# A fused retention and gated-experts kernel: the norm's last step on ScalarE, the masked scores in front of the normalised rows, operand tasks open to two engines, zero matmuls between the first scores

## The chip, the cores and the metric

The kernel runs on one core of one Trainium2 chip. The core has TensorE (PE in the profile; its weight loads are the separate row PEld), VectorE (DVE), ScalarE (ACT), GpSimd (POOL) and SyncE (SP, which issues most DMAs here). The metric is the device time of one execution in microseconds; lower is better. The kernel before was timed in three runs: 880.64, 884.82 and 885.79 us, median 884.82.

## The reference

Three stages, one after the other. Only the first stage and its passage to the second are touched by the change.

```
state = gamma * state + k[t] v[t]^T          # 2 batches, 8 heads, 768 steps, head_dim 64
y[t]  = scale * q[t] state

x  = y as (1536 tokens, 512)
xn = x / sqrt(mean(x*x) + 1e-6) * rms_g
x  = (silu(xn @ w_gate) * (xn @ w_val)) @ w_out           # 512 -> 1536 -> 512

p   = domain_probs / (sum(domain_probs) + 1e-9)           # 4 experts
out = sum over e of p[:, e] * (relu(x @ w1[e]) @ w2[e])   # 512 -> 1024 -> 512
```

## The kernel before

**Stage one, the retention.** A batch of 768 steps is cut into 6 chunks of 128; the two batches give 12 chunks, 0 to 11. For each chunk `scores` (L600) makes the 128x128 products of k and q for 8 heads into two PSUM banks. `masked` (L608, on DVE) multiplies them with decay and causality into the tile am. `mix` adds two products in one bank: q with the carried state S (L620, not in the first chunk of a batch) and am with v (L628). It then updates the state on PE (L654, operand kn scaled at L578 on POOL or DVE) and copies it to S on ACT (L661). The scaling of q (L589) is a task of POOL or DVE too.

**The norm.** In `mix`, ACT squares the 128x512 result with a running sum ss (L640), takes r0 = sqrt(ss/512 + eps) (L642) and vv = ss/512 + eps (L644). In `normal`, DVE takes r1 = 1/r0 (L668) and improves it by one Newton step, r1 * (1.5 - 0.5 * vv * r1 * r1), in three instructions on one column (L671 to L673). In `normal2`, DVE makes the normalised rows xn = y * r1 * rms_g (L680). `to_x` has PE transpose xn (L702) and lets ACT, DVE and POOL turn the result into operands of stage two.

**The passage to stage two.** Every float32 operand of stage two is split into a high part (a cast on ACT) and a low part (a subtraction on POOL or DVE), and each product is three matmuls: hi*hi, hi*lo, lo*hi (L447). Stage two is done by a 2x2 block scheme with 7 products, so that sums of blocks are wanted as well (tsum, L724 to L736). The operand tiles are xX, xB22 and xT, each with a hi and a lo tile. A group of chunks 0 to 5 feeds token half 0, chunks 6 to 11 token half 1. Weights arrive as 64-bit floats and are turned into float32 by ACT (L299) and DVE (L302 to L320), summed (L336) and split (L364, L369) by ACT, DVE and POOL.

**What sets the order.** There is no automatic scheduling here: the program writes out each engine's queue. Work that is not bound to a place is a task of the class Pace, which holds estimated costs and engine clocks. `pace.fill(span)` issues waiting tasks that its estimate says would end within the span; `pace.need(task)` issues a task now. A task names the engines that it may run on: "P" is POOL, "PV" is POOL or DVE, whichever the estimate has free first. Once issued, each engine runs its queue strictly in the order written. Loads are issued on SP in program order, behind the buffers that they refill (q and v have 3 buffers, k and kn 2).

**One iteration i of the main loop** loads chunk i+2, does `normal` and `normal2` of chunk i-1, `scores` and `masked` of chunk i+1, a fill, `mix` of chunk i, a fill, `to_x` of chunk i-1 and a last fill. The last two chunks are normalised directly behind their own mix. In iteration 10 the first products of stage two stand on PE behind `to_x` of chunk 9. Before the loop, 8 matmuls on zeros (L772, into the bank called idle) run while the first loads are under way.

Of the kernel before, what the change touches and what calls it, by code (L numbers as in the profile page):

```python
# [7 lines left out]
F32 = mybir.dt.float32  # L8
# [3 lines left out]
AF = mybir.ActivationFunctionType  # L12
ALU = mybir.AluOpType
PSUM = bass.MemoryType.PSUM

P = 128
# [3 lines left out]
EPS = 1e-6  # L20
# [131 lines left out]
def tile_retention_gated_experts(  # L152
# [27 lines left out]
    nc = tc.nc  # L180
    B, NCH = qt.shape[:2]
    H = c_k.shape[2]
    S = NCH * CHUNK
    NT, DM = out.shape
    DFF = w_gate.shape[1]
    E, _, F = w1.shape
    D = DM // H
    NTT = NT // P
    NP = H // 2
# [33 lines left out]
    pace = Pace({"A": nc.scalar, "V": nc.vector, "P": nc.gpsimd, "D": nc.sync})  # L223
# [311 lines left out]
    with ExitStack() as actx:  # L535
        ac = actx.enter_context(tc.tile_pool(name="ac", bufs=1))
# [9 lines left out]

        rows = [wstage.tile([P, H, CHUNK], F32, tag="wst", name=f"rows{x}")[0:1] for x in range(2)]
        g_sb = ac.tile([P, DM], F32, name="g_sb")
        eps = ac.tile([P, 1], F32, name="eps")
        table = ac.tile([P, 1], F32, name="table")  # L550

        S_sb = [ac.tile([P, NP, CHUNK], F32, name=f"S{x}") for x in range(2)]
# [2 lines left out]
        NS = len(chunks)  # L555
# [55 lines left out]
        def mix(i):  # L611
            b, c = chunks[i]
            yf = bank()
            if c:
                pace.matmuls(0, pace.need(st[i]["q task"]))
            y = yf.rearrange("p (h d) -> p h d", h=H)
            vt, am = st[i]["v"].rearrange("p (h d) -> p h d", h=H), st[i]["am"]
            for n in range(NP):
# [8 lines left out]
                for j in range(2):  # L627
# [4 lines left out]
                        start=not c,  # L632
                        stop=(j == 1) or not c,
                    )
            pace.matmuls(2.53 if c else 1.65, st[i]["v end"], st[i]["am end"], st[i].get("S end", 0.0))
            xn = ap2.tile([P, DM], F32, tag="xn", name="xn")
            ss, vv, r0, r1, r2 = (
                ap2.tile([P, 1], F32, tag=nm, name=nm) for nm in ("ss", "vv", "r0", "r1", "r2")
# [2 lines left out]
            end = pace.did("A", DM + 100)  # L641
            nc.scalar.activation(out=r0, in_=ss, func=AF.Sqrt, scale=1.0 / DM, bias=eps)  # L642
            end = pace.did("A", 1, end)
            nc.scalar.activation(out=vv, in_=ss, func=AF.Identity, scale=1.0 / DM, bias=eps)  # L644
            pace.did("A", 1)
            if c + 1 < NCH:

                if c == 0:
                    st[i]["state"] = pairs(psum_sum.tile([P, 512], F32, name="state"))
                d = st[i]["state"]  # L650
                pace.matmuls(0, pace.need(st[i]["k task"]))
                ks, vs = pairs(st[i]["kn"]), pairs(st[i]["v"])
                for n in range(NP):
                    nc.tensor.matmul(  # L654
                        out=d[:, n, :], lhsT=ks[:, n, :], rhs=vs[:, n, :], start=(c == n == 0), stop=True,
                        skip_group_check=True,
                    )
                pace.matmuls(0.87)
                new = S_sb[c % 2]
                for r in (slice(0, D), slice(D, P)):  # L660
                    nc.scalar.copy(out=new[r, :, r], in_=d[r, :, r])  # L661
                    s_end = pace.did("A", DM // 2)
                st[i + 1]["state"], st[i + 1]["S"], st[i + 1]["S end"] = d, new, s_end
            st[i]["norm"] = yf, xn, ss, vv, r0, r1, r2, end

        def normal(i):
            yf, xn, ss, vv, r0, r1, r2, end = st[i]["norm"]
            nc.vector.reciprocal(out=r1, in_=r0)  # L668
            end = pace.did("V", 1, end)

            nc.vector.scalar_tensor_tensor(out=r2, in0=r1, scalar=vv, in1=r1, op0=ALU.mult, op1=ALU.mult)  # L671
            nc.vector.tensor_scalar(out=r2, in0=r2, scalar1=-0.5, scalar2=1.5, op0=ALU.mult, op1=ALU.add)
            nc.vector.tensor_tensor(out=r1, in0=r1, in1=r2, op=ALU.mult)  # L673
            for _ in range(3):
                end = pace.work("V", 1, end)
            st[i]["r"] = xn, yf, r1, end

        def normal2(i):
            xn, yf, r1, end = st[i]["r"]
            nc.vector.scalar_tensor_tensor(out=xn, in0=yf, scalar=r1, in1=g_sb, op0=ALU.mult, op1=ALU.mult)  # L680
            st[i]["xn"], st[i]["xn end"] = xn, pace.did("V", DM, end)
# [4 lines left out]
        def split(g, readers, dep, hi, lo, t, size, last=False):  # L686

            high = pace.add(1, "A", size, lambda eng: eng.copy(out=hi, in_=t), dep)
            low = pace.add(
                1, "PV" if last else "P", size,  # L690
                lambda eng: eng.tensor_tensor(out=lo, in0=t, in1=hi.bitcast(F32), op=ALU.subtract), [high],
            )
            readers += [high, low]
            x_tasks[g] += [high, low]

        def to_x(i):
# [8 lines left out]
            if blk == 0:  # L705
# [22 lines left out]
            nc.vector.tensor_tensor(out=lo, in0=b22, in1=hi.bitcast(F32), op=ALU.subtract)  # L728
            pace.did("V", DM // 2, end)
            third = pace.add(  # L730
                1, "PV" if i == NS - 1 else "P", DM // 2,
                lambda eng: eng.tensor_tensor(out=t3, in0=t2, in1=b1[:, 0:KH], op=ALU.subtract), [done],
            )
            fourth = pace.add(
                1, "PV" if i == NS - 1 else "P", DM // 2,
                lambda eng: eng.tensor_tensor(out=t4, in0=b1[:, KH:KD], in1=t2, op=ALU.subtract), [done],  # L736
            )
            first_block[b, "readers"] += [third, fourth]
# [4 lines left out]
        def early(i):  # L743
            return i >= NS - 2

        man = tc.manual_schedule()
        man.__enter__()
        nc.gpsimd.memset(eps, EPS)

        nc.scalar.activation(out=table, in_=eps, func=AF.Sqrt)  # L750
        for x in range(2):
# [36 lines left out]
        for i in range(NS):  # L788
# [13 lines left out]
                nc.sync.dma_start(out=p_raw, in_=probs.rearrange("(t p) e -> p t e", p=P))  # L802
            if i and not early(i - 1):
                normal(i - 1)
                normal2(i - 1)
            if i + 1 < NS:
                scores(i + 1)
                masked(i + 1)
                pace.fill(1.15)
            mix(i)  # L810
            pace.fill(2.53)
            if i + 2 < NS:
                load(i + 2, "kn")
            if early(i):
# [326 lines left out]
```

## Time and profile before

| | us |
|---|---|
| median of 3 runs | 884.82 |
| lowest and highest run | 880.64, 885.79 |
| the profiled execution, whole | 882.98 |
| its span, first to last instruction | 881.2 |
| PE busy | 857.9 (97%) |
| PEld, DVE, ACT, POOL busy | 800.5, 593.5, 359.7, 296.2 |
| mean granted clock of TensorE | 0.981 |

The profile is of one execution. "Busy" is time in which an engine has an instruction in work; a wait is charged to what released it. The granted clock is the share of full speed that TensorE had: 1.00 is 2.4 GHz, 0.50 is 1.2 GHz. Between 0 and 112 us of the span lie the retention and the passage to stage two; after that PE is nearly always busy.

### The profile page before, as it was taken

How to read it: one execution, taken by the hardware profiler on the slowest of the kernel's cores; microseconds unless marked ns; L12 is line 12 of the kernel's file. 1: busy time of each engine (PE TensorE's matmuls, PEld its weight loads, DVE VectorE, ACT ScalarE, POOL GpSimd, SP SyncE). 2: the span in 40 equal slices, each digit the busy share in tenths (PEclk: the TensorE clock that was granted, in tenths of full speed). 3: DMA queues.
4: the chain of work that ended last, by engine and by line, in shares of the span. 5: the costliest groups of instructions: out<-in, count | busy, mean ns of one | idle time of the engine just before them, and what ended most of it. 6: DMA issues, size and time to landing. Idle time of an engine off the chain costs nothing.

```text
span 881.2 us, 12572 instructions
## 1 busy us (share of the span) xinstructions
PE 857.9 (97%) x4710; PEld 800.5 (91%) x4710; DVE 593.5 (67%) x1093; ACT 359.7 (41%) x786; POOL 296.2 (34%) x365
## 2 busy tenths in 40 slices
PE   9996899999999999999999999999999999999998
PEld 8886899999999999989899998899998899988997
DVE  3989789999788774872655566565656556565554
ACT  1654545545354544665342333333233333333221
POOL 2755534536374655951220120122112012111000
PEclk7978899999999999999999999999999999999999
DMA  7842022223121210010111010011011001101003
GB/s 277 286 151 85 25 72 79 89 72 96 49 86 59 73 48 25 25 37 13 48 37 35 26 48 26 23 49 36 13 47 49 25 25 49 36 13 48 25 1 144
DMA packets 33410, 53.96 MB, mean 61 GB/s; under 512 B 4419, under 2 KB 13507, under 8 KB 33349
## 3 DMA queue, kind: packets, MB, share of 16 engines
q1 hardware_dynamic: 33200, 53.01, 18.9%
q8 instruction: 37, 0.61, 0.3%
q14 instruction: 25, 0.20, 0.1%
q10 hardware_dynamic: 148, 0.14, 0.0%
HBM read 50.00 MB, written 3.15 MB: 60 GB/s over the span
## 4 chain that ended last, share of the span: by engine, by line
PE 82%; DVE 11%; POOL 3%; ACT 2%; issue 2%; DMA 1%; SPq 0%; DVEq 0%; ACTq 0%
PE bank L447 39%; PE bank L1022 10%; PE bank L1023 10%; PE bank L1021 10%; PE bank L955 3%; PE bank L954 3%; PE bank L953 3%; PE bank L628 1%; DVE s L880 1%; DVE sums L336 1%; DVE top L320 1%; POOL x2Tlo L906 1%; DVE kept L877 1%; DVE am L608 1%; DVE widelo L369 1%
## 5 line engine op out<-in xcount | busy, mean ns | idle before, releaser
L1029 DVE SCALAR_TENSOR_TENSOR oacc<-bank,p_sb,oacc 128x512 f32<-128x512 f32 (+1 forms) x181 | 134.9, 746 | 66.5 <-PE bank L1023 66.5
L1023 PE MATMUL bank<-plainhi,hs 128*128 128x512 f32 (+1 forms) x386 | 151.1, 391 | 0.0
L1022 PE MATMUL bank<-plainlo,hs 128*128 128x512 f32 (+1 forms) x386 | 151.0, 391 | 0.0
L1021 PE MATMUL bank<-plainhi,hs 128*128 128x512 f32 (+1 forms) x386 | 149.7, 388 | 0.0
L456 ACT COPY kept<-bank 128x384 f32<-128x384 f32 x168 | 80.4, 479 | 158.3 <-PE bank L447 156.6
L986 DVE TENSOR_TENSOR kept<-bank,kept 128x384 f32<-128x384 f32 x96 | 53.5, 558 | 119.1 <-PE bank L447 89.1
L369 POOL TENSOR_TENSOR plainlo<-wst,plainhi 128x512 fp32r<-128x512 f32 x16 | 27.8, 1739 | 283.3 <-ACT plainhi L364 283.3
L369 POOL TENSOR_TENSOR widelo<-sums,widehi 128x512 fp32r<-128x512 f32 x40 | 52.0, 1300 | 120.9 <-ACT widehi L364 118.3
L447 PE MATMUL bank<-x2Thi,widehi 128*128 128x384 f32 x256 | 86.4, 338 | 0.7 <-DVE kept L986 0.7
L447 PE MATMUL bank<-x2Thi,widelo 128*128 128x384 f32 x256 | 86.4, 337 | 0.0
L1023 PEld LDWEIGHTS bank<-plainhi,hs 128*128 128x128 f32 x386 | 72.4, 188 | 15.0
L447 PE MATMUL bank<-x2Tlo,widehi 128*128 128x384 f32 x256 | 86.0, 336 | 0.0
L1022 PEld LDWEIGHTS bank<-plainlo,hs 128*128 128x128 f32 x386 | 72.4, 188 | 14.0 <-POOL plainlo L369 0.3
L1021 PEld LDWEIGHTS bank<-plainhi,hs 128*128 128x128 f32 x386 | 72.6, 188 | 13.6
L989 ACT ACTIVATE hs<-kept 128x384 fp32r<-128x384 f32 x96 | 50.4, 525 | 76.6 <-DVE kept L986 76.6
L447 PE MATMUL bank<-xThi,widehi 128*128 128x384 f32 x192 | 65.3, 340 | 3.3 <-ACT kept L456 3.0
L954 PE MATMUL bank<-hlo,plainhi 128*128 128x384 f32 x192 | 64.4, 335 | 1.1 <-POOL hlo L885 1.0
L955 PE MATMUL bank<-hhi,plainlo 128*128 128x384 f32 x192 | 64.3, 335 | 0.9 <-DVE plainlo L369 0.9
L447 PE MATMUL bank<-xThi,widelo 128*128 128x384 f32 x192 | 64.6, 337 | 0.0
L447 PE MATMUL bank<-xTlo,widehi 128*128 128x384 f32 x192 | 64.6, 337 | 0.0
L953 PE MATMUL bank<-hhi,plainhi 128*128 128x384 f32 x192 | 64.2, 334 | 0.0
L993 DVE SCALAR_TENSOR_TENSOR hs<-kept,hs 128x384 fp32r<-128x384 f32 x96 | 53.0, 563 | 4.1 <-ACT hs L989 4.1
(144 smaller groups left out, 1936.7 us busy)
## 6 DMA issues: line engine op xcount, KB each, us to landing
wst<-in_moe_w_dram SPq DMA_DIRECT2D x64, 256.0 KB, 2.7
wst<-in_moe_w_gate_dram SPq DMA_DIRECT2D x12, 512.0 KB, 3.7
wst<-in_moe_w_val_dram SPq DMA_DIRECT2D x12, 512.0 KB, 3.8
wst<-in_moe_w_out_dram SPq DMA_DIRECT2D x12, 512.0 KB, 3.3
v<-in_vn_dram SPq DMA_DIRECT2D x12, 256.0 KB, 4.7
kn<-in_kn_dram SPq DMA_DIRECT2D x12, 256.0 KB, 2.7
q<-in_qt_dram SPq DMA_DIRECT2D x11, 256.0 KB, 4.2
k<-in_kt_dram SPq DMA_DIRECT2D x11, 256.0 KB, 3.9
```

What stands on the lines that cost most here:

```text
L369: eng.tensor_tensor(out=at(lo), in0=t, in1=at(hi).bitcast(F32), op=ALU.subtract)
L447: nc.tensor.matmul(out=ps, lhsT=lhs, rhs=rhs, start=(first and j == i == 0), stop=(j == KH - 1 and i == 2), skip_group_check=not first,)
L456: nc.scalar.copy(out=t, in_=ps)
L953: nc.tensor.matmul(out=ps, lhsT=whi[:, c], rhs=hi, start=(f == 0), stop=False)
L954: nc.tensor.matmul(out=ps, lhsT=whi[:, c], rhs=lo, start=False, stop=False)
L955: nc.tensor.matmul(out=ps, lhsT=wlo[:, c], rhs=hi, start=False, stop=(f == NF - 1))
L986: nc.vector.tensor_tensor(out=t, in0=a, in1=t, op=ALU.add)
L993: lambda eng: eng.scalar_tensor_tensor(out=lo, in0=t, scalar=0.0, in1=hi.bitcast(F32), op0=ALU.max, op1=ALU.subtract), [high],
L1021: nc.tensor.matmul(out=ps, lhsT=hi[:, c], rhs=whi[:, cols], start=(f == 0), stop=False)
L1022: nc.tensor.matmul(out=ps, lhsT=hi[:, c], rhs=wlo[:, cols], start=False, stop=False)
L1023: nc.tensor.matmul(out=ps, lhsT=lo[:, c], rhs=whi[:, cols], start=False, stop=(f == NF - 1))
L1029: nc.vector.scalar_tensor_tensor(out=acc, in0=ps, scalar=pe, in1=acc, op0=ALU.mult, op1=ALU.add)
```

## The change

Five edits.

- The Newton step moves from three DVE instructions to three ACT instructions: a square of r1, an affine step with vv as its scale (vv now holds -0.5 * (ss/512 + eps), with the bias tiles less and more), and a product. The reciprocal stays on DVE.
- In iteration i, `normal2` of chunk i-1 comes behind `scores` and `masked` of chunk i+1 and no longer in front of them.
- The low parts and block sums of the operands of stage two may go to POOL or DVE for all chunks; before, only those of chunk 11 could.
- In iteration 0, eight matmuls on zeros stand between the scores of chunk 0 and those of chunk 1.
- The estimate of `mix` is spread over its head pairs, with fills between them, and the fills after it are shorter.

```diff
-        eps = ac.tile([P, 1], F32, name="eps")
+        eps, less, more = (ac.tile([P, 1], F32, name=nm) for nm in ("eps", "less", "more"))
 ...
+            pace.matmuls(0, st[i]["v end"], st[i]["am end"], st[i].get("S end", 0.0))
             y = yf.rearrange("p (h d) -> p h d", h=H)
 ...
-            pace.matmuls(2.53 if c else 1.65, st[i]["v end"], st[i]["am end"], st[i].get("S end", 0.0))
+                pace.matmuls(0.65 if c else 0.45)
+                if n + 1 < NP:
+                    pace.fill(0.65 if c else 0.45)
 ...
-            nc.scalar.activation(out=vv, in_=ss, func=AF.Identity, scale=1.0 / DM, bias=eps)
-            pace.did("A", 1)
+            nc.scalar.activation(out=vv, in_=ss, func=AF.Identity, scale=-0.5 / DM, bias=less)
+            pace.did("A", 100)
 ...
                 pace.matmuls(0.87)
+                pace.fill(0.65)
 ...
             nc.vector.reciprocal(out=r1, in_=r0)
             end = pace.did("V", 1, end)
 
-            nc.vector.scalar_tensor_tensor(out=r2, in0=r1, scalar=vv, in1=r1, op0=ALU.mult, op1=ALU.mult)
-            nc.vector.tensor_scalar(out=r2, in0=r2, scalar1=-0.5, scalar2=1.5, op0=ALU.mult, op1=ALU.add)
-            nc.vector.tensor_tensor(out=r1, in0=r1, in1=r2, op=ALU.mult)
-            for _ in range(3):
-                end = pace.work("V", 1, end)
+            nc.scalar.activation(out=r0, in_=r1, func=AF.Square)
+            nc.scalar.activation(out=r2, in_=r0, func=AF.Identity, scale=vv, bias=more)
+            nc.scalar.activation(out=r1, in_=r1, func=AF.Copy, scale=r2)
+            end = pace.work("A", 420, end)
 ...
             low = pace.add(
-                1, "PV" if last else "P", size,
+                1, "PV", size,
 ...
             third = pace.add(
-                1, "PV" if i == NS - 1 else "P", DM // 2,
+                1, "PV", DM // 2,
 ...
             fourth = pace.add(
-                1, "PV" if i == NS - 1 else "P", DM // 2,
+                1, "PV", DM // 2,
 ...
-        nc.gpsimd.memset(eps, EPS)
+        for t, value in ((eps, EPS), (less, -0.5 * EPS), (more, 1.5)):
+            nc.gpsimd.memset(t, value)
 ...
             if i and not early(i - 1):
                 normal(i - 1)
-                normal2(i - 1)
+            if i == 0:
+
+                for n in range(8):
+                    nc.tensor.matmul(out=idle[:, 0, :], lhsT=S_sb[0][:, 0, :], rhs=S_sb[0][:, 0, :], start=True, stop=True)
             if i + 1 < NS:
                 scores(i + 1)
                 masked(i + 1)
-                pace.fill(1.15)
+            if i and not early(i - 1):
+                normal2(i - 1)
+            pace.fill(1.15)
             mix(i)
-            pace.fill(2.53)
+            pace.fill(0.87)
```

How the queues move, at three places. First PE from the start to the state update of chunk 0, before:

```order
L772 MATMUL bank<-S_115 128x128 x8
L778 MATMUL bank<-rows_111,rows_110 128x128 x8
L600 MATMUL bank<-q,k 128x128 x16
L628 MATMUL bank<-v,am 128x64 x8
L654 MATMUL state<-v,kn 128x128 x4
```

and PE at the same place in the changed kernel (S_117 is the same state tile of zeros):

```order
L776 MATMUL bank<-S_117 128x128 x8
L782 MATMUL bank<-rows_111,rows_110 128x128 x8
L600 MATMUL bank<-q,k 128x128 x8
L812 MATMUL bank<-S_117 128x128 x8
L600 MATMUL bank<-q,k 128x128 x8
L629 MATMUL bank<-v,am 128x64 x8
L657 MATMUL state<-v,kn 128x128 x4
```

Eight zero matmuls now stand between the scores of chunk 0 and of chunk 1; the rest of PE's queue in the retention keeps its order. Second, DVE around the norm of chunk 9, whose rows xn the transposes in front of stage two's first products read, before:

```order
L369 TENSOR_TENSOR widelo_738<-sums,widehi_737 128x4x128
L369 TENSOR_TENSOR widelo_738<-top,widehi_737 128x2x128
L369 TENSOR_TENSOR widelo_738<-top,widehi_737 128x128
L336 TENSOR_TENSOR sums<-top 128x128
L336 TENSOR_TENSOR sums<-sums,top 128x128
L336 TENSOR_TENSOR sums<-top,sums 128x128
L302 SCALAR_TENSOR_TENSOR wst<-bits,wst 128x512
L668 RECIPROCAL r_877<-r_876 128x1
L671 SCALAR_TENSOR_TENSOR r_878<-r_877,vv 128x1
L672 TENSOR_SCALAR r_878<-r_878 128x1
L673 TENSOR_TENSOR r_877<-r_877,r_878 128x1
L680 SCALAR_TENSOR_TENSOR xn<-bank,r_877,g_sb 128x512
```

(one more row of L336 stood between, alike the first) and in the changed kernel, from the norm of chunk 8 to what follows that of chunk 10:

```order
L683 SCALAR_TENSOR_TENSOR xn<-bank,r_813,g_sb 128x512
L672 RECIPROCAL r_878<-r_877 128x1
L608 TENSOR_TENSOR am<-bank,mask 128x512 x2
L683 SCALAR_TENSOR_TENSOR xn<-bank,r_878,g_sb 128x512
L672 RECIPROCAL r_937<-r_936 128x1
L683 SCALAR_TENSOR_TENSOR xn<-bank,r_937,g_sb 128x512
L727 TENSOR_TENSOR tsum<-bank,first 128x256
L729 TENSOR_TENSOR tsum<-bank,tsum 128x256
L731 TENSOR_TENSOR xB22lo_91<-bank,xB22hi_90 128x2x128
L739 TENSOR_TENSOR tsum<-first,tsum 128x256
L320 SCALAR_TENSOR_TENSOR top<-wst,bits 128x512
```

No weight instruction stands any more between the masked scores of one chunk and the norm of the next; the sums and splits of that weight come later or are POOL's. Third, ACT around the norm of chunk 10, before:

```order
L640 ACTIVATE xn,ss<-bank 128x512
L642 ACTIVATE r_945<-ss,eps 128x1
L644 ACTIVATE vv<-ss,eps 128x1
L661 COPY S_115<-state 64x4x64 x2
L722 CAST xB22hi_90<-bank 128x2x128
L456 COPY kept<-bank 128x384
```

and in the changed kernel:

```order
L643 ACTIVATE xn,ss<-bank 128x512
L645 ACTIVATE r_936<-ss,eps 128x1
L647 ACTIVATE vv<-ss,less 128x1
L665 COPY S_117<-state 64x4x64 x2
L675 ACTIVATE r_936<-r_937 128x1
L676 ACTIVATE r_938<-r_936,more,vv 128x1
L677 ACTIVATE r_937<-r_937,r_938 128x1
L725 CAST xB22hi_90<-bank 128x2x128
L456 COPY kept<-bank 128x384
```

The three new instructions stand behind the copies of the state and in front of the next operand casts; the first of them reads the reciprocal that DVE makes, so ACT's queue stands until DVE has come to it.

## Rows read from the trace of the kernel before

**Rows 1.** Stretches: width, busy time and instructions by engine, clock, DMA.
```profile
20.00:46.00 26.00, 23.15 (x227) 21.85 (x226) 21.86 (x46) 16.53 (x45) 18.46 (x22) 1.00 0.86 284
46.00:57.00 11.00, 11.00 (x65) 10.05 (x66) 9.64 (x21) 4.03 (x11) 4.97 (x5) 0.53 0.23 73
...
77.50:88.00 10.50, 4.24 (x17) 4.11 (x16) 10.12 (x17) 3.16 (x9) 5.46 (x5) 0.67 0.00 0
...
102.00:112.00 10.00, 6.99 (x25) 6.67 (x23) 6.97 (x14) 4.70 (x10) 6.02 (x7) 0.66 0.01 2
...
130.00:881.00 751.00, 743.76 (x3897) 692.10 (x3895) 494.75 (x898) 297.76 (x633) 230.14 (x294) 1.00 0.15 46
```

**Rows 2.** PE's waits, 0 to 125 us: in total, times, longest.
```profile
PE bank L702 <- DVE xn L680: 8.6, 3, 6.3
PE bank L447 <- ACT kept L456: 3.0, 1, 3.0
...
PE bank L600 <- DMA q<-in_qt_dram: 1.4, 1, 1.4
```

**Rows 3.** Two stretches of 1 us (columns as Rows 1): where the clock changed.
```profile
9.00:10.00 1.00, 1.00 (x10) 1.00 (x12) 0.87 (x2) 0.00 (x0) 0.20 (x1) 0.54 0.53 182
...
19.00:20.00 1.00, 1.00 (x9) 1.00 (x9) 1.00 (x2) 0.00 (x0) 1.00 (x1) 0.84 0.98 330
```

**Rows 4.** PE in time: start, duration, line, count, [idle before, releaser].
```profile
8.98 2.02 PE L600 MATMUL bank<-q,k 64*128 64x128 f32 x16 [0.45 <-DMA k<-in_kt_dram]
11.07 3.85 PE L628 MATMUL bank<-v,am 128*128 128x64 f32 x16
14.71 2.02 PE L654 MATMUL state<-v,kn 128*128 128x128 f32 x8
...
23.18 1.16 PE L600 MATMUL bank<-q,k 64*128 64x128 f32 x16
...
27.00 1.11 PE L654 MATMUL state<-v,kn 128*128 128x128 f32 x8
...
28.48 1.16 PE L600 MATMUL bank<-q,k 64*128 64x128 f32 x16
...
35.23 1.16 PE L600 MATMUL bank<-q,k 64*128 64x128 f32 x16 [1.38 <-DMA q<-in_qt_dram]
...
45.97 0.63 PE L702 MATMUL bank<-square,xn 128*128 128x128 f32 x4 [1.46 <-DVE xn L680]
```

**Rows 5.** DVE in time: a sum of weight blocks twice, chunk 9's xn, masked scores.
```profile
54.31 0.29 DVE L336 TENSOR_TENSOR sums<-top 128x128 f32<-128x128 f32 x1
...
75.39 1.38 DVE L336 TENSOR_TENSOR sums<-top 128x128 f32<-128x128 f32 x1
...
83.08 0.75 DVE L680 SCALAR_TENSOR_TENSOR xn<-bank,r,g_sb 128x512 f32<-128x512 f32 x1
83.75 1.28 DVE L608 TENSOR_TENSOR am<-bank,mask 128x512 f32<-128x512 f32 x2
```

**Rows 6.** POOL in time: low parts of operands, beside the two long waits.
```profile
75.28 3.90 POOL L691 TENSOR_TENSOR xTlo<-tsum,xThi 128x512 fp32r<-128x512 f32 x3
...
100.42 3.32 POOL L691 TENSOR_TENSOR xTlo<-tsum,xThi 128x512 fp32r<-128x512 f32 x2
```

**Rows 7.** Lines of the norm, 10 to 100 us: count, busy us, mean ns.
```profile
L673 DVE TENSOR_TENSOR r<-r,r 128x1 f32<-128x1 f32 x12 | 6.1, 504 | 0.4
L671 DVE SCALAR_TENSOR_TENSOR r<-r,vv 128x1 f32<-128x1 f32 x12 | 4.6, 385 | 0.9
L672 DVE TENSOR_SCALAR r<-r 128x1 f32<-128x1 f32 x12 | 1.8, 154 | 0.4
...
L642 ACT ACTIVATE r<-ss,eps 128x1 f32<-128x1 f32 x12 | 3.5, 294 | 0.4
```

**Rows 8.** ACT in time, at the end of the second long wait.
```profile
104.45 0.62 ACT L688 CAST xThi<-tsum 128x512 fp32r<-128x512 f32 x1 [3.43 <-POOL tsum L736]
```

**Rows 9.** DMA issues: count, KB each, us from issue to landing.
```profile
q<-in_qt_dram SPq DMA_DIRECT2D x11, 256.0 KB, 4.2
```

## The prediction

> **What bounds the kernel now.** I read the stretches first. From 130 us to the end PE is busy 743.76 of 751.00 us at full clock [rows 1], and the change leaves PE's queue there as it was. What can be gained lies in the first 112 us: in PE's waits and in the stretches where TensorE was granted 1.2 GHz instead of 2.4. The list of PE's waits up to 125 us gives the first: 8.6 us in three waits on the normalised rows xn, the longest 6.3; 3.0 us on an ACT copy; 1.4 us on a load of q [rows 2]; 0.45 us on one of k at the start [rows 4]. The clock gives the second: it falls just after 9 us and returns just after 19 [rows 3]; a clock of 0.53 over the 11 us from 46 means about 10.3 us at half speed; and 77.5 to 88 us and 102 to 112 us stand at 0.67 and 0.66 [rows 1]. What half speed costs is seen by like rows: the same scores take 2.02 and 1.16 us, the same state update 2.02 and 1.11 [rows 4]. So a microsecond of PE work at half clock is some 0.55 us at full clock, and 0.45 is to be had back.
>
> Who holds PE up is seen on DVE. It is busy 21.86 of the 26 us from 20 to 46, and 10.12 of 10.50 around the longest wait [rows 1]. There it makes block sums that take 1.38 us each, while the same instruction takes 0.29 us elsewhere [rows 5]; POOL is at that moment in three operand subtractions of 3.90 us together [rows 6], so these small DVE instructions stretch to about POOL's length. Chunk 9's xn stands behind them at 83.08 [rows 5].
>
> **The change, part by part.**
>
> *The Newton step.* It takes 504 + 385 + 154 ns, 1.04 us a chunk and 12.5 us in all, off DVE [rows 7]. On ACT I price three one-column instructions at 294 ns, the row for a like one [rows 7]: 0.88 us a chunk, 10.6 us in all. ACT is busy 16.53 of 26 us in the fullest stretch [rows 1], so that hides in its idle time. The new wait: ACT's queue stands until the reciprocal is made, and behind it wait the operand casts and, once they are late, the next chunk's square and state copy.
>
> The Trainium skill speaks against this part: the page "ScalarE: Activation LUTs", section "Rules for kernel authors", puts additions and multiplications on VectorE and not on ScalarE. By the same page's "What ACT_TABLE_LOAD costs" (186 ns for a small ACTIVATE, some 93 more for each pointer operand) the three would be 0.84 us by my estimate, and the trace's 294 ns for the square root with a bias agrees with that. Rows 7 do not bear the rule out for this DVE, where the step took 1.04 us; what it would do here is the third rival below.
>
> *Masked scores in front of xn.* A chunk takes 5.30 us at full clock (scores at 23.18 and 28.48), of which the scores are 1.16 [rows 4]. PE reaches the transposes of the chunk before last only at the end of that period, so DVE has about 4.1 us after the scores for the two masked products, 1.28 us, and xn, 0.75 us [rows 5]. This leaves 2.1 us of slack, and the written order has no weight work there for the last chunks. I therefore let all three waits on xn go: **8.6 us**. Next in line are the loads.
>
> *Clock, 46 to 57 us.* The half-speed stretch begins right after PE idled 1.46 us for xn [rows 4]. Without that wait 10.3 x 0.45 = 4.6 us are to be had; a wait of the same length on a load would undo it. Ends 0 and 4.6, and I take **3.2**, nearer the upper end, because the only load wait of that length there was, 1.38 us for q before the scores at 35.23 [rows 4], lies in a stretch whose clock stayed at 1.00 [rows 1].
>
> *Clock, 77.5 to 88 us.* Most of the 4.24 us of PE work there ran at half speed, after the long wait [rows 1]. Without the wait: 3.6 x 0.45 = **1.6**.
>
> *The zeros.* Eight of them are twice the four state matmuls: 2.2 us at full clock, 4.0 at half [rows 4]; they fill the wait of 0.45 us. If the clock then holds, the ten slow microseconds [rows 3] give 4.5, so 4.5 + 0.4 - 2.2 = +2.7. If it falls all the same and returns no sooner, 0.4 - 4.0 = -3.6. [...] Idle time alone cannot have brought the fall at 9 us: only 0.45 us stand before it, and 1.4 us on q did nothing. So I don't take the upper end but **+1.5**.
>
> *Operand tasks on either engine.* The written order sends one scaling of kn, four block sums and a few low parts to DVE, no more. That shortens POOL's chain where the second token half is finished: 3.32 us of low parts there [rows 6], then a sum, then the ACT cast at 104.45 that followed 3.43 us of waiting for POOL [rows 8], then PE. The wait of 3.0 us and the half-speed stretch after it (about 6 us of work, 2.7 us) make 5.7 together. But ACT now also has Newton steps, and DVE has sums and splits of a weight in front of chunk 11's reciprocal. Ends 0 and 5.7; I take **1.5**, nearer nothing.
>
> *New waits.* Loads are issued when PE frees their buffers and take 4.2 us to land [rows 9], against a chunk of 5.30 us, with four or five loads to be issued in it. Where PE used to stand for other reasons, from 46 to 57 us, the weights' loads now compete: I expect two waits of about 1 us. Chunk 11's xn behind weight work may cost 1 to 2 us at its transposes. Ends 0 and -6; I take **-3**.
>
> The two fills of constants on POOL, the copies' order and the pace's estimates cost nothing by themselves: POOL has no data yet at the start. Behind 130 us nothing is counted, since PE bounds there.
>
> **Sum.** 8.6 + 3.2 + 1.6 + 1.5 + 1.5 - 3 = 13.4 us. The profiled execution took 882.98, so 869.6; the median of the runs stands 1.8 above that execution, so **871**. The ends: everything held, 8.6 + 4.6 + 1.6 + 2.7 + 5.7 with the load wait of 1.4 gone too, is 24.6 and gives 860; the unknowns all at their low ends, 8.6 + 0 + 1.6 - 3.6 + 0 - 6, is 0.6 and gives 884.
>
> **Rivals.**
>
> 1. *Given back at the passage to stage two.* PE arrives some 14 us sooner, but the second half's operands and the next weights come when DVE, ACT and POOL have made them. For it: DVE was busy 10.12 of 10.50 us, and POOL still ran 3.32 us of low parts at the end [rows 1, 6]. Against it: 12.5 us leave DVE. Term "either engine" 0, new waits -6: 8.9 us, **876**.
> 2. *The zeros don't do what they are for.* The clock falls anyway, at the start and in the narrow first chunk of the second batch (its like took 3.85 us at half speed [rows 4]). Then -3.6 and 0 stand for +1.5 and 3.2: a gain of 5.1, **880**. For it: the fall at 9 us after so little idle time. [...]
> 3. *Slower: the norm becomes late in most chunks.* ACT waits for a reciprocal that stands behind DVE's weight work, squares the next chunk late, and xn misses the 2.1 us of slack. It decides where a late xn idles PE by about 1.5 us, as the wait of 1.46 us did before the clock fell [rows 4]. Such a chunk then runs at half speed: 5.30 / 0.55 = 9.6 us, so 4.3 + 1.5 = 5.8 lost. Four such chunks lose 23 against the 13.4 gained: **894**. This is also what the skill's rule on ScalarE would come to. Against it: the room on ACT, and no weight work before xn in the last chunks.
>
> **Chances.** My forecast 0.66, the rivals 0.16, 0.13 and 0.05. A measurement of this kernel tells about 1% (9 us) from no change, which puts the lines at 876 and 894. Of the forecast's share nine tenths lie below 876, of the first rival's a half; with a little of the second this is 0.71 for faster by over 1%, 0.24 for within 1%, and 0.05 for slower. The range that holds it 8 times in 10 runs from 861, nearly all terms at their good ends, to 880, which takes in the first rival and half of the second.
>
> **What would show it.** In the profile after: no wait of PE on xn over 1 us up to chunk 10, and transposes of chunk 9 right behind the state update of chunk 10 (the 8.6). Clock 1.00 from the first scores to 20 us, or a fall at about 9 us with the zeros at 0.25 us a record (the zeros). Clock 1.00 through the first chunk of the second batch (the 3.2). A wait on q or k of about 1 us in chunks 7 to 9, and one on xn at the last transposes (the -3). The wait on the second half's operands, 3.0 us now, shrunk or moved earlier by as much as PE (the 1.5). The prediction fails if PE waits on xn in several chunks, or if PE, arriving sooner, waits longer at 88 to 112 us than it did, so that the expert stage begins less than 10 us sooner.

## The result: 872.47 us, a gain of 1.4%

The changed kernel took 872.47 us in the median of four runs (870.64 to 873.68), the kernel before 885.31 beside it (880.64 to 887.82). The ratio is 0.9859, with a 95% interval of 0.9813 to 0.9905. The ratios, here and in the table below, leave out the runs that were put down as slow, and they are not the quotients of the two medians. The forecast was 871, within 861 to 880. In 77 later runs, on three chips, the kernel before had a median of 881.68, so these four runs (and the three that the forecast starts from, 884.82) lie some 3 us high. Timed again, the changed kernel took 872.99 beside 882.20, a ratio of 0.9897 (0.9865 to 0.9928): about 1%, some 9 us. The profiled execution took 870.64 us, its span 868.9, at a mean granted clock of 0.996; before, these were 882.98, 881.2 and 0.981. The first product with w_out starts at 102.47 us and no longer at 116.69, so the front of the kernel is 14.2 us shorter; 12.3 of these are left at the end of the span. Of the 12.3, 7.4 us are PE's busy time (857.9 to 850.5) and 4.9 its idle time (23.3 to 18.4).

### The profile page after: what moved, and what is told of

It reads as the page before. It is cut to its first block, busy times and chain, and to the rows that moved or that the text cites. A ratio compares the mean times of both kernels' runs of the same rounds, so it can differ in the third digit from the quotient of the medians.

```text
span 868.9 us, 12593 instructions
## 1 busy us (share of the span) xinstructions
PE 850.5 (98%) x4726; PEld 791.6 (91%) x4726; DVE 571.8 (66%) x1038; ACT 368.5 (42%) x822; POOL 309.7 (36%) x386
## 4 chain that ended last, share of the span: by engine, by line
PE 82%; DVE 9%; POOL 4%; ACT 3%; issue 2%; DVEq 0%; ACTq 0%; POOLq 0%
PE bank L447 39%; PE bank L1031 10%; PE bank L1032 10%; PE bank L1030 10%; PE bank L963 3%; PE bank L964 3%; PE bank L962 3%; DVE s L889 2%; DVE top L320 1%; PE bank L629 1%; POOL x2Tlo L915 1%; DVE kept L886 1%; DVE sums L336 1%; PE bank L600 1%; DVE wst L302 1%
## 5 line engine op out<-in xcount | busy, mean ns | idle before, releaser
L369 POOL TENSOR_TENSOR plainlo<-wst,plainhi 128x512 fp32r<-128x512 f32 x16 | 27.8, 1739 | 283.3 <-ACT plainhi L364 283.3
L369 POOL TENSOR_TENSOR widelo<-sums,widehi 128x512 fp32r<-128x512 f32 x42 | 54.5, 1299 | 116.0 <-ACT widehi L364 113.5
L1030 PEld LDWEIGHTS bank<-plainhi,hs 128*128 128x128 f32 x386 | 72.5, 188 | 13.6
L894 POOL TENSOR_TENSOR hlo<-s,hhi 128x384 fp32r<-128x384 f32 x44 | 47.5, 1085 | 28.9 <-ACT hhi L891 28.8
```

The source lines that it names most:

```text
L369: eng.tensor_tensor(out=at(lo), in0=t, in1=at(hi).bitcast(F32), op=ALU.subtract)
L1030: nc.tensor.matmul(out=ps, lhsT=hi[:, c], rhs=whi[:, cols], start=(f == 0), stop=False)
```

## The profile after

PE's waits from 0 to 125 us, the view of [rows 2]:

```profile
PE bank L447 <- ACT kept L456: 4.7, 2, 4.1
PE bank L776 <- DVE S L760: 1.5, 1, 1.5
PE bank L621 <- ACT S L665: 1.4, 1, 1.4
PE bank L600 <- DMA q<-in_qt_dram: 1.3, 2, 1.0
PE bank L705 <- DVE xn L683: 0.2, 1, 0.2
```

The 8.6 us on xn are down to 0.2. The largest wait is now 4.1 us on kept, ACT's copy of a half-finished bank of stage two: only when it is made does PE add the next product in that bank; and there is a new one of 1.4 us on ACT's copy of the state S. (The 1.5 us on S at L776 lie before any data are there, in both kernels.) The stretches, columns as in [rows 1]; the first line is the kernel before, the others the changed one:

```profile
57.00:77.50 20.50, 19.61 (x188) 18.50 (x187) 18.35 (x34) 13.25 (x34) 12.92 (x13) 1.00 0.59 192
...
46.00:57.00 11.00, 8.53 (x84) 7.56 (x83) 7.77 (x15) 8.90 (x27) 10.21 (x12) 1.00 0.69 231
57.00:77.50 20.50, 20.50 (x183) 19.92 (x183) 10.04 (x20) 14.11 (x41) 17.11 (x18) 1.00 0.28 88
77.50:88.00 10.50, 6.40 (x29) 5.99 (x29) 7.98 (x17) 6.95 (x18) 6.24 (x7) 0.84 0.07 26
...
102.00:112.00 10.00, 10.00 (x59) 9.79 (x58) 9.57 (x22) 5.07 (x11) 5.87 (x9) 1.00 0.44 143
```

The clock of 46 to 57 us went from 0.53 to 1.00, that of 102 to 112 from 0.66 to 1.00. From 57 to 77.5 us PE has no idle time, and DVE (the third busy time) is in work for 10.04 of 20.5 us; before it was 18.35. After 20 us only 77.5 to 88 us stays below full clock; from 0 to 20 us the mean is 0.91, because the clock is 0.50 under the zeros. PE in time, to be set against [rows 4]:

```profile
6.96 1.16 PE L600 MATMUL bank<-q,k 64*128 64x128 f32 x16
8.05 3.68 PE L812 MATMUL bank<-S 128*128 128x128 f32 x16
11.66 1.16 PE L600 MATMUL bank<-q,k 64*128 64x128 f32 x16
...
21.18 1.16 PE L600 MATMUL bank<-q,k 64*128 64x128 f32 x16 [0.17 <-PE bank L705]
...
48.10 1.16 PE L600 MATMUL bank<-q,k 64*128 64x128 f32 x16 [0.97 <-DMA q<-in_qt_dram]
...
56.09 0.46 PE L621 MATMUL bank<-S,q 128*128 128x128 f32 x2 [1.38 <-ACT S L665]
...
82.29 0.45 PE L447 MATMUL bank<-xB22hi,widehi 128*128 128x384 f32 x1 [4.10 <-ACT kept L456]
```

The scores of chunk 3 start at 21.18 us, before at 23.18: 2.0 us sooner. At chunk 8 it is 48.10 against 54.74, 6.6 sooner; at the transposes of chunk 9, 70.33 against 83.89, 13.6 sooner. The wait of 4.10 us takes some of that back. Behind it stands ACT's queue, here from the norm of chunk 11 on:

```profile
78.79 0.28 ACT L647 ACTIVATE vv<-ss,less 128x1 f32<-128x1 f32 x1
80.65 0.20 ACT L675 ACTIVATE r<-r 128x1 f32<-128x1 f32 x1 [1.58 <-DVE r L672]
...
81.30 0.29 ACT L677 ACTIVATE r<-r,r 128x1 f32<-128x1 f32 x1
81.50 0.35 ACT L725 CAST xB22hi<-bank 128x256 fp32r<-128x256 f32 x1
81.76 0.86 ACT L456 COPY kept<-bank 128x384 f32<-128x384 f32 x2
```

and DVE at the same time:

```profile
77.03 1.58 DVE L694 TENSOR_TENSOR xTlo<-tsum,xThi 128x512 fp32r<-128x512 f32 x1
78.54 0.68 DVE L369 TENSOR_TENSOR widelo<-sums,widehi 128x512 fp32r<-128x512 f32 x1
79.14 0.88 DVE L369 TENSOR_TENSOR widelo<-top,widehi 128x256 fp32r<-128x256 f32 x2
...
80.46 0.16 DVE L672 RECIPROCAL r<-r 128x1 f32<-128x1 f32 x1
81.63 0.75 DVE L683 SCALAR_TENSOR_TENSOR xn<-bank,r,g_sb 128x512 f32<-128x512 f32 x1 [1.02 <-ACT r L677]
```

The copy that PE waits for needs nothing from the norm. It only stands behind three Newton instructions, and these behind a reciprocal that DVE makes after a low part and the splits and sums of a weight.

## The experiments

Theory A: xn in time, by the two edits of the norm, makes the gain. Theory B: the either-engine tasks make it. Theory C: the zeros make it, by the clock. "Ratio" is to the kernel before on the same chip, with its 95% interval. The chips differ: one for e1 to e4, one for the changed kernel again, z1, i1 and i2, one for u2, m3, p1 and i3. A microsecond or two between medians of different chips shows nothing by itself. Edits are against the changed kernel unless said otherwise. Each profile is of one execution: those of e1, e3, u2 and i3 are the slowest of their runs, those of e4 and m3 the second slowest, those of the changed kernel, z1 and i1 the fastest.

| kernel | norm's edits | finer fills | either engine | zeros | median us | ratio |
|---|---|---|---|---|---|---|
| changed | yes | yes | yes | yes | 872.47 | 0.9859 (0.9813 to 0.9905) |
| changed, again | yes | yes | yes | yes | 872.99 | 0.9897 (0.9865 to 0.9928) |
| e1 | yes | yes | yes | - | 876.16 | 0.9947 (0.9918 to 0.9976) |
| e2 | rows moved only | yes | yes | yes | 874.24 | 0.9946 (0.9910 to 0.9982) |
| e3 | Newton only | yes | yes | yes | 873.51 | 0.9934 (0.9904 to 0.9964) |
| e4 | yes | yes | - | yes | 877.79 | 0.9973 (0.9935 to 1.0010) |
| u2 | - | yes | yes | yes | 869.80 | 0.9892 (0.9852 to 0.9932) |
| m3 | yes | yes | - | - | 878.38 | 0.9990 (0.9959 to 1.0020) |
| z1 | - | - | - | yes | 881.80 | 0.9987 (0.9965 to 1.0009) |
| p1 | - | - | yes | - | 884.70 | 1.0062 (1.0032 to 1.0092) |

The kernel before had medians of 882.06 (e1 to e4), 882.20 (the changed one again, z1, and i1 and i2 below) and 880.54 (u2, m3, p1, and i3 below).

### One part undone at a time

**e1, no zeros.**

```diff
-            if i == 0:
-
-                for n in range(8):
-                    nc.tensor.matmul(out=idle[:, 0, :], ...)
```

> The changed kernel without the eight zero matmuls between the first scores; everything else as changed. Theory A (the gain is that xn no longer stands late on DVE, by the moved Newton step and the moved masked scores): the zeros cut the half-clock stretch at the start from about 10 us to 3.4 us but cost 3.7 us themselves, so 1 to 3 us are lost: 874 to 876 us. Theory B (operand tasks on either engine make the gain): within 2 us of the changed kernel, 871 to 875. Theory C (the zeros and the clock make the gain): over 878, with half clock from about 9 to 19 us and perhaps a second slow stretch at the second batch.

It took 876.16 us, some 3.5 more than the changed kernel, just above A's range and below C's. Its largest wait of PE:

```profile
PE bank L600 <- DMA q<-in_qt_dram: 4.5, 3, 2.7
```

The stretch of 0 to 20 us has a clock of 0.74, as before the change, and the loads of q are waited for longer (1.3 us in the changed kernel).

**e2, the Newton step back on DVE**, in its three instructions (vv has its old sign and bias again, too; the edit is shown in part).

```diff
 ...
-            nc.scalar.activation(out=r0, in_=r1, func=AF.Square)
-            nc.scalar.activation(out=r2, in_=r0, func=AF.Identity, scale=vv, bias=more)
-            nc.scalar.activation(out=r1, in_=r1, func=AF.Copy, scale=r2)
+            nc.vector.scalar_tensor_tensor(out=r2, in0=r1, scalar=vv, in1=r1, op0=ALU.mult, op1=ALU.mult)
+            nc.vector.tensor_scalar(out=r2, in0=r2, scalar1=-0.5, scalar2=1.5, op0=ALU.mult, op1=ALU.add)
+            nc.vector.tensor_tensor(out=r1, in0=r1, in1=r2, op=ALU.mult)
```

> The changed kernel with the Newton step back on DVE, three instructions, the rest as changed. Theory A: DVE takes back some 12 us of one-column work, ScalarE no longer stands for the reciprocal: 875 to 880, with waits of PE on xn over 1 us in some chunks, but the 1.4 us wait on the state copy at chunk 8 and most of the 4.1 us wait on the kept copy at 78 us gone. Theory B: within 2 us of the changed kernel, 871 to 875. Theory C: the same as B. A fourth possibility: faster than the changed kernel by 2 to 5 us, if the waits that ScalarE's queue made cost more than DVE's relief gave.

**e3, xn in front of scores and masked again.**

```diff
                 normal(i - 1)
+                normal2(i - 1)
 ...
                 masked(i + 1)
-            if i and not early(i - 1):
-                normal2(i - 1)
```

> The changed kernel with xn in front of the scores and masked scores again, the rest as changed. Theory A: the masked scores wait for xn and so for the Newton step on ScalarE; am is late by under a chunk, which is hidden, but DVE idles for ScalarE in each chunk: 874 to 880. Theory B and C: within 2 us of the changed kernel, 871 to 875.

874.24 and 873.51 us: against the two medians of the changed kernel each alone is worth 0.5 to 1.8 us, which is not clear of the noise: both ratios' intervals overlap with that of the changed kernel timed again. B and C expected these times. In e2 the waits on xn are back at 5.2 us, in four waits, the last long one at 57.82 us; in e3 they are 1.1 us. None of the 6.3 us of [rows 2], in front of chunk 9's transposes, is back in either.

**e4, operand tasks on POOL only** (but for the last chunk; one of the two block sums is shown).

```diff
-                1, "PV", size,
+                1, "PV" if last else "P", size,
 ...
-                1, "PV", DM // 2,
+                1, "PV" if i == NS - 1 else "P", DM // 2,
```

> The changed kernel with the operand tasks (low parts and block sums) of all chunks but the last bound to POOL again, the rest as changed. Theory A: few of these went to DVE anyway (one scaling, some sums and low parts), so 872 to 876, with the passage to stage two a little later by POOL. Theory B: the gain goes, 880 to 886, with POOL busy without a break from 60 to 100 us and PE waiting for its low parts. Theory C: within 2 us of the changed kernel.

877.79 us, 5 more than the changed kernel: the part that costs most when it is taken out. That is between A's range and B's. PE in time, the two waits on kept:

```profile
83.99 0.69 PE L447 MATMUL bank<-xB22hi,widehi 128*128 128x384 f32 x1 [2.62 <-ACT kept L456]
...
97.75 0.69 PE L447 MATMUL bank<-xB22hi,widehi 128*128 128x384 f32 x1 [2.65 <-ACT kept L456]
```

The second is of the kind of the 3.0 us of [rows 2], in front of another product; the changed kernel's second wait on kept is 0.6 us. Both records take 0.69 us, where 0.44 is full speed, and 77.5 to 102 us stand at clocks of 0.78 and 0.74. So e4 decides for neither, e2 and e3 speak against A as it was put, and no single part holds the whole gain. The parts were therefore also tried alone.

### Parts alone, and the norm undone as a whole

The changed kernel itself, once more:

> The changed kernel as it is, timed on the same chip as the other runs of this call, so that each can be set against it. From its first timing I expect 871 to 874 us and a spread of the runs of under 5 us; the kernel before spread over 15 us in the first four experiments. If the gain hangs on where the clock happens to fall, this kernel should spread as widely as the one before.

872.99 us, spread over 2.9 us (871.44 to 874.38), where the kernel before spread over 9.6 (878.62 to 888.24).

**z1, the zeros alone**, in the kernel before:

```diff
+            if i == 0:
+                for n in range(8):
+                    nc.tensor.matmul(out=idle[:, 0, :], lhsT=S_sb[0][:, 0, :], rhs=S_sb[0][:, 0, :], ...)
             if i + 1 < NS:
                 scores(i + 1)
```

> The kernel before with the eight zero matmuls between the scores of chunks 0 and 1 as its only change. Theory C (the zeros and the clock carry a good part of the gain by themselves): the half-clock stretch at the start shrinks from 10 us to 3.5, and the time is 3 to 5 us below the kernel before (877 to 879 where that gives 882). Theory A (the waits on xn carry it): PE comes to chunk 6 and to the rows xn of chunk 9 sooner by what the zeros gave, waits there longer by the same, and the clock falls there as before: less than 2 us gained, 880 to 883, with 8 us or more of waits on xn in the list.

No gain. PE's waits on xn stay at 6.2 us (8 or more were expected):

```profile
PE bank L702 <- DVE xn L680: 6.2, 4, 1.9
```

and in the stretch from 57 to 77.5 us DVE (the third busy time) is as full as before the change, 19.15 us:

```profile
57.00:77.50 20.50, 18.59 (x138) 17.37 (x137) 19.15 (x40) 12.07 (x32) 7.90 (x7) 0.75 0.44 148
```

C falls as a theory of the whole gain.

**p1, either engine alone**, in the kernel before (e4's edit the other way round):

> The kernel before with the operand tasks open to both engines as its only change. Theory B (they carry a gain by themselves, as the 4 to 5 us lost when they were taken from the changed kernel suggest): 877 to 879 where the kernel before gives 882. Theory A (DVE is full in the kernel before, and only the norm's edits make room): the tasks stand in front of xn on DVE, waits on xn of 8 us or more, and the time within 2 us of the kernel before, or above it.

Slower, by 0.3 to 0.9%. B, as a gain of that part alone, falls too. The second expectation was right on the time. The norm is late in six chunks, but by 4.5 us in all and not by the 8 or more expected, by PE's waits:

```profile
PE bank L702 <- DVE xn L680: 4.5, 6, 1.8
```

and the same stretch reads:

```profile
57.00:77.50 20.50, 18.63 (x173) 17.14 (x173) 19.81 (x38) 14.36 (x38) 7.78 (x9) 1.00 0.46 143
```

With the old, coarse fills the planner sends the tasks to a DVE that is already full (19.81 us), and POOL, the fifth busy time, has 7.78 us of work in 20.5.

**m3, the norm's edits and the finer fills**, without zeros and either engine (the edits of e1 and e4 together):

> The kernel before with the two edits of the norm alone (Newton step on ScalarE, masked scores in front of xn, the fills that go with them): no zeros, operand tasks on POOL only. Theory A (xn in time makes the gain): waits on xn under 2 us, and 4 to 7 us below the kernel before, 875 to 878 where that gives 882, with the clock still half for 7 to 10 us at the start. Rival 'the parts only pay together': PE comes sooner and waits for POOL's operands instead, with kept and S waits of 6 us or more, and less than 3 us are gained.

878.38 us; its ratio is no gain that can be measured. The wait on xn is 0.2 us, and yet others took its place:

```profile
PE bank L447 <- ACT kept L456: 5.2, 2, 2.6
PE bank L600 <- DMA q<-in_qt_dram: 4.3, 3, 2.4
```

The time is what the rival said ("the parts only pay together"), with waits on kept and q where it named kept and S. xn in time is not enough.

**u2, both edits of the norm undone** (e2 and e3 together); zeros, either engine and finer fills stay:

> The changed kernel with both edits of the norm undone: Newton step on DVE, xn in front of the masked scores; zeros, either-engine tasks and fills stay. Undoing one alone cost 0.5 and 1.2 us against the changed kernel. Theory A with the two as substitutes (either one alone brings xn in time): with both gone the waits on xn come back, 5 us or more, and the time is 877 to 880. Rival (fills and the either-engine tasks already keep DVE's weight work away from xn): waits on xn under 3 us and 873 to 875.

869.80 us, 867.54 to 871.21: no slower than the changed kernel that can be measured (0.9892 to the kernel before, where that had 0.9859 and 0.9897). Theory A, with its 877 to 880, falls, and the rival's 873 to 875 was too high as well. The waits:

```profile
PE bank L447 <- ACT kept L456: 3.4, 2, 2.4
PE bank L706 <- DVE xn L684: 2.1, 3, 1.7
```

What brought xn forward is suggested by DVE's lines of the weights, L302 to L369, from 60 to 82 us (busy us, mean ns, idle before). In u2 there are two instructions, 1.4 us:

```profile
L302 DVE SCALAR_TENSOR_TENSOR wst<-bits,wst 128x512 f32<-128x512 f32 x1 | 0.7, 692 | 0.2 <-ACT bits L299 0.2
L320 DVE SCALAR_TENSOR_TENSOR top<-wst,bits 128x512 uint32<-128x512 uint32 x1 | 0.7, 675 | 0.0
```

In the kernel before the same lines hold 14 instructions there and 11.9 us, the stretched sums of [rows 5] among them:

```profile
L336 DVE TENSOR_TENSOR sums<-top 128x128 f32<-128x128 f32 x2 | 2.7, 1362 | 0.0
L369 DVE TENSOR_TENSOR widelo<-top,widehi 128x256 fp32r<-128x256 f32 (+1 forms) x4 | 2.3, 624 | 1.4 <-ACT widehi L364 1.4
...
```

The other kernels without the finer fills hold 9.5 (z1) and 5.7 us (p1) there, the changed kernel 3.6 and m3 1.5. The work is not gone: from 82 to 112 us it is 11.0 us on DVE in u2 against 4.9 before, and POOL has 16.7 us of it up to 112 us against 7.0. So in u2 DVE waits for the norm, and no longer the norm for DVE:

```profile
68.54 0.16 DVE L672 RECIPROCAL r<-r 128x1 f32<-128x1 f32 x1 [1.91 <-ACT r L645]
```

The finer fills are what all kernels with a light DVE share: from 57 to 77.5 us it is busy 18.35, 19.15 and 19.81 us without them (before, z1, p1) and 7.4 to 15.7 with them (all the others), whatever else is in or out. That is an argument by elimination: the fills alone were not run, nor the zeros and either engine together without them.

### Better than the change

**i1, chunk 11's Newton step on DVE**, in two instructions:

```diff
+            if i == NS - 1:
+                nc.vector.scalar_tensor_tensor(out=r2, in0=r1, scalar=vv, in1=r1, op0=ALU.mult, op1=ALU.mult)
+                nc.vector.scalar_tensor_tensor(out=r1, in0=r2, scalar=1.5, in1=r1, op0=ALU.add, op1=ALU.mult)
+                ...
+                return
             nc.scalar.activation(out=r0, in_=r1, func=AF.Square)
```

> The changed kernel with the Newton step of chunk 11 alone on DVE, in two instructions instead of three on ACT. In the changed kernel PE waits 4.1 us at 78 us on the copy kept on ACT, which stands behind the three Newton instructions of chunk 11, and those wait 1.6 us for a reciprocal that DVE makes late. Theory 'queue of ACT': the copy no longer stands behind the reciprocal, so the 4.1 us shrink to 2.5 or less and the half-clock stretch behind them goes: 869 to 871 where the changed kernel gives 872.5. Rival 'PE is simply early': the operands of token half 1 are late whatever ACT does, the wait moves to another of them (xT, xB22 or their low parts), and the time is within 1 us of the changed kernel.

869.42 us (868.51 to 869.87), ratio 0.9854 (0.9823 to 0.9884); no run of it is as slow as the fastest of the changed kernel beside it, on the same chip. ACT in time:

```profile
78.92 0.28 ACT L647 ACTIVATE vv<-ss,less 128x1 f32<-128x1 f32 x1
79.10 0.35 ACT L732 CAST xB22hi<-bank 128x256 fp32r<-128x256 f32 x1
79.36 0.86 ACT L456 COPY kept<-bank 128x384 f32<-128x384 f32 x2
```

and PE, its waits and the first product with w_out (L969 here):

```profile
79.89 0.44 PE L447 MATMUL bank<-xB22hi,widehi 128*128 128x384 f32 x1 [1.58 <-ACT kept L456]
...
90.67 0.44 PE L447 MATMUL bank<-xB22hi,widehi 128*128 128x384 f32 x1 [1.85 <-ACT kept L456]
...
100.15 0.33 PE L969 MATMUL bank<-hhi,plainhi 128*128 128x384 f32 x1
```

The copy follows at once, and w_out's products begin at 100.15 and not 103.19 (the changed kernel on that chip). The stretch behind the wait, in the changed kernel on that chip and then in i1:

```profile
77.50:88.00 10.50, 6.40 (x26) 5.99 (x25) 8.20 (x16) 5.78 (x17) 5.31 (x7) 0.67 0.09 38
...
77.50:88.00 10.50, 8.79 (x48) 7.54 (x47) 9.99 (x23) 7.61 (x20) 6.63 (x8) 1.00 0.13 40
```

The planner also moved six products on xT and two block sums of that chunk, so that the whole 3.6 us cannot be put down to the copy. What is shown is that the one wait of 4.1 us became three, 4.0 in total (1.58 and 1.85 the longest), and that the clock stayed at 1.00 behind them. In sum PE waits for kept as long as it did; in these profiles the clock is the larger part of what was won.

**i2, i1 without the fills of the last iteration.**

```diff
-                if n + 1 < NP:
+                if n + 1 < NP and i < NS - 1:
                     pace.fill(0.65 if c else 0.45)
 ...
-            pace.fill(1.15)
+            if i < NS - 1:
+                pace.fill(1.15)
             mix(i)
-            pace.fill(0.87)
+            if i < NS - 1:
+                pace.fill(0.87)
```

> As the run before (Newton step of chunk 11 on DVE), and besides no fill inside the last iteration's mix or around it, so that on DVE the reciprocal and the rows xn of chunk 11 stand right behind the state products of their chunk, and weight sums and low parts come after them. Theory 'the reciprocal stands behind weight work on DVE': xn of chunk 11 is made 2 to 3 us sooner, no wait on kept over 1.5 us is left and the time is 867 to 870. Rival 'the weights are the next in line': what was put off is w_out's and the expert's split, PE waits on plainlo, widehi or widelo by the 2 to 3 us won, and the time is that of the run before or longer.

874.15 us, 4.7 more than i1. The rival holds: the weight that was put off is waited for, by PE's list.

```profile
PE bank L447 <- ACT widehi L364: 3.5, 1, 3.5
```

**i3, the Newton step of chunks 3, 4, 5, 6 and 11 on DVE**, with i1's two instructions and nothing else moved.

> The changed kernel with the Newton step of chunks 3, 4, 5, 6 and 11 on DVE in two instructions, of the others on ScalarE; no other instruction moves against the run that had chunk 11 alone there (869.4 us). In that run ScalarE still stood 5.2 us for DVE's reciprocal in these four chunks, and PE waited 1.2 us for the copy of the state behind it at 56 us. Theory 'ScalarE should not stand for DVE': that wait of 1.2 us on S and those of ScalarE on the reciprocal go, 868 to 869. Rival 'PE is held there by the loads': the microsecond goes into the wait on q, 869 to 870.

872.05 us (869.11 to 877.32), which neither theory expected. The profile is of the execution that took 877.32. The wait on S is gone, but PE's list has two others,

```profile
PE bank L718 <- DVE xn L696: 2.4, 3, 1.3
PE bank L600 <- ACT widehi L364: 2.1, 1, 2.1
```

and of the lines from 10 to 100 us (busy us, mean ns, idle before) this is the step's last instruction in chunks 3 to 6:

```profile
L684 DVE SCALAR_TENSOR_TENSOR r<-r,r 128x1 f32<-128x1 f32 x4 | 2.9, 718 | 0.1
```

On DVE the one-column product took 718 ns in these chunks, 160 ns in chunk 11, and 295 ns on ACT in the changed kernel. In that execution ACT no longer waits there, and xn is late instead; whether that holds in the faster ones is not shown.

i1 and u2 are the fastest kernels found, 869.4 and 869.8 us, on two chips. In both, chunk 11's Newton step is not on ACT, so nothing of the norm's second half stands in front of kept. That alone does not make a kernel fast: e2, i2 and i3 have it as well, at 874.24, 874.15 and 872.05 us.

## Why the prediction was right, and where it was not

**The number and the places.** 872.47 lies 1.5 us from the forecast. That it is so near is in part luck: the forecast starts from a median some 3 us above that of the 77 later runs, and two terms were wrong by 2.4 and 3.5 us in opposite directions (below). The gain forecast was 13.4 us; beside more runs it is about 9. Waits on xn 8.6 to 0.2; clock 0.53 to 1.00 from 46 to 57 us; two waits on q (0.32 and 0.97 us; two of about 1 us were expected); w_out 14.2 us sooner.

**The step that failed: who brings xn forward.** The prediction gave the 8.6 us to the masked scores in front of xn, with 12.5 us taken off DVE by the norm, and said that the pace's estimates cost nothing by themselves. u2 undoes both edits of the norm and loses nothing that can be measured, with 2.1 us of waits on xn; z1 and p1 lack the finer fills and keep 6.2 and 4.5 us. So the edits that were given the 8.6 us are not needed for the gain: that is shown. What remains is the line that was costed at nothing, the estimates and fills, which by elimination moved the weight work from in front of the norm of chunks 8 to 10 (11.9 us before, 1.4 in u2). The order of the queues did show that no weight work was left there; the mistake was to read it as the effect of the edits beside it.

**Terms.** *Clock 46 to 57 us*, 3.2: from the scores of chunk 7 to those of chunk 8 took 8.22 us before and 5.79 after, a gain of 2.4 with 0.97 of load wait inside, so 3.4. *Clock 77.5 to 88 us*, 1.6: the lead went from 7.1 us at the scores of chunk 11 to 13.6 at the transposes of chunk 9, the whole long wait; but the half speed came back behind the new wait, and this stretch stood at 0.84 (0.67 when timed again), so this term was not had. *Zeros*, 1.5: the clock fell under them (they took 3.68 us) and was back for the scores at 11.66 us, between the two ends of the prediction. In the profiles that start as early as that of before, the scores of chunk 3 come at 21.0 to 21.8 us with zeros (five) and 22.7 to 23.2 without (three), so about 1.5; where the start is late (below) it is 23.3 to 24.4 with zeros (five) and 22.4 without (one), so there they cost about as much. That would explain z1's nought; how its other runs started is not known. *Either engine*, 1.5: mis-sized. Beside the finer fills and the zeros it is worth 5 us (e4), near the upper end of 5.7: e4 has two waits on kept of 2.6 us and slow stretches behind them, which fits the reason given there. Without the zeros it is about 2 (m3 against e1, two chips), and with the coarse fills it loses 4 (p1). *New waits*, -3: too small. q 1.3, the state copy 1.4 and kept 4.1 make 6.8, of which the 1.4 on q of the kernel before must be taken off: 5.4, near the low end of -6. Chunk 11's xn was expected 1 to 2 us late at its transposes, and the loss came through ACT's queue.

**The rivals.** Something of the first came true: PE came early to the passage to stage two and gave 4.7 us back on kept. The third, slower, did not come, but its mechanism did, in one chunk: ACT stood for a reciprocal behind DVE's weight work and PE paid 4.1 us. The Trainium skill, page "ScalarE: Activation LUTs", section "Rules for kernel authors", wants additions and multiplications on VectorE. For that chunk i1 agrees (869.42 against 872.99 us, ratios 0.9854 and 0.9897); for chunks 3 to 6 besides, i3 does not (872.05, ratio 0.9929).

**How much is clock.** In 77 runs of the kernel before, the mean granted clock had a median of 0.988, in the six of the changed kernel beside z1 0.996. Twice the missing share times 880 us is the time at half speed, 21 and 7 us; the 14 us between at 0.45 make 6.3, of a gain of about 9 in these runs. That is an estimate, and rough, since the column does not show every slow stretch (below). In the first pair of profiles it was 7.4 us less busy time of 12.3, the work of the zeros included. The rest is idle time of PE.

**Open.** Whether the finer fills alone give the gain, or zeros and either engine together would without them; neither was run. Every variant re-plans the queues, and single undos of 1 to 2 us (e2, e3) lie within what that moves.

## What to carry to other kernels

Read who moved a late instruction from the whole queue in front of it, not from the edit next to it: a planner's estimate may be the edit that matters. When parts pay only together, single undos understate and single additions mislead, so try both. An instruction that needs another engine's answer should not stand in front of a copy that PE waits for (i1); for chunks 3 to 6 of this kernel, taking it away brought no gain (i3). Set a change against many runs of the kernel before: four of them put the gain 3 to 4 us too high.

## What the runs showed of the hardware

The same queue of PE, up to the first scores, starts in two ways. In some profiles PE runs at full speed from about 5 us and drops later (0.54 from 9 to 10 us in [rows 3]); in six others, the kernel before's queue with zeros (z1) among them, the first scores come at 8.87 us and take nearly twice their time (2.08 for 1.16), while the granted clock is given as 1.00. PE in time, from z1:

```profile
8.87 2.08 PE L600 MATMUL bank<-q,k 64*128 64x128 f32 x16
10.88 3.50 PE L808 MATMUL bank<-S 128*128 128x128 f32 x16
14.30 1.16 PE L600 MATMUL bank<-q,k 64*128 64x128 f32 x16
```

and a stretch of 1 us of it, the clock in the third column from the end:

```profile
9.00:10.00 1.00, 1.00 (x10) 1.00 (x12) 0.70 (x2) 0.00 (x0) 0.18 (x1) 1.00 1.03 307
```

So the column does not show every slow stretch; the length of a known record does. The kernel before spread from 870.4 to 888.2 us in 77 runs, wider than the whole gain, and its fastest run is as fast as the changed kernel; but only 6 of the 77 lie below 874.4 us, the slowest of the changed kernel's ten.
